# Load order, ScalarE-issued first weight rows and a reordered normalisation loop at the start of an attention plus token-mixing-MLP kernel

## The chip, the cores and the metric

The kernel runs on one core of one Trainium2 chip. The metric is the device time of one execution in microseconds; the number used is the median of several runs. A separate profiled execution gives the trace that is read here. Its span (first to last instruction on the core) is a little shorter than its device time.

## What is computed

The input is `x`, 2048 tokens of 1024 features in bf16. The reference normalises it to `xn`, and returns `x` plus a segmented attention of `xn` (4 segments of 512 tokens, 32 heads, a softmax part and a memory part, mixed by a gate) plus a token-mixing MLP. Only the MLP's first half matters for the change:

```
xn = _layernorm(x, axis=-1)
h  = _layernorm(xn, axis=-1)
u  = jnp.einsum('bsd,sf->bdf', h, w1) + b1      # contraction over the 2048 tokens, f = 3584
u  = gelu(u)
y  = jnp.einsum('bdf,fs->bds', u, w2) + b2
out = x + attention(xn) + transpose(y)
```

Each token's mean and variance over its 1024 features are therefore needed before that token can take part in the first product, and every output of that product needs all tokens.

## The kernel before

Tokens lie on the 128 partitions, in 16 chunks of 128 (`N_TCH`). The work is issued in this order (L571 to L577): `loads`, `warm`, `norm_and_first_hidden`, `hidden`, `over_late`, `attention_and_out`. Engines run their own instruction streams in order; a wait stands in the stream of the engine that waits, so whatever is behind it on that engine waits too.

**First stage (about the first 39 us).** For chunk c the kernel loads `xin[:, c, :]` (256 KB) and the 128 rows of `w1first` that belong to it (512 columns, 128 KB), computes the statistics, writes the normalised `h[:, c, :]`, and runs eight matmuls of 128x512 into eight PSUM banks (4 column blocks of w1, `N_EARLY`, by 2 halves of the features). Chunk c is the c-th term of the contraction, so the matmuls must follow the chunks and TensorE can go no faster than `h` appears.

- `loads` (L715) issues all transfers from SP's queue, in the order they are to land: x0, x1, w1-0, x2, w1-1, x3, w1-2 and 3, x4 and 5, w1-4 and 5, the two bias rows `brow`, and so on in pairs; then `beta_sb` and the first full weight slot `w1slot[2]`. `load_w1` (L743) uses the default issuer of `FW.dma` (L226), which is SP.
- `warm` (L748) clears a tile, lets GpSimd fill `mhalf` with -0.5 (the exponent for the power), runs one tiny gelu on ScalarE, which brings in its table, and lets TensorE run 14 dummy matmuls (`N_WARM`).
- `stats` (L784): the odd chunks (`ACT_STATS`) take their sums on ScalarE, by two passes (L793 mean, L795 mean square). The even chunks take them on VectorE: `bn_stats` of features 0 to 511 (L800, part 0), of 512 to 1023 (L802), and `bn_aggr` (L804), the last two being part 1.
- `scale` (L807): GpSimd turns this into the reciprocal root `ln_r2`: two small operations (L814, L816) and a power (L821) for an odd chunk, one (L819) and the power for an even one. Chunk 0 has L819 on VectorE.
- `ln_h` (L824) on VectorE: `h = (x - mean) * rs` (L829).
- `norm_and_first_hidden` (L761) writes the order out by hand. In each even turn c VectorE's stream is: L800 of chunk c+2, `ln_h(c+1)`, L802 and L804 of chunk c+2, `ln_h(c+2)`. GpSimd's stream is `scale(c+1)`, `scale(c+2)`.
- `bias_columns` (L846) turns the bias rows into columns by eight 32x32 transposes (L851) and a copy (L852), all in one go in turn 10.

**Second stage**, `hidden` (L907), to about 212 us: gelu of the eight early banks on ScalarE (L941), then 48 groups of 16 matmuls for the other 24 column blocks, each with w1 in slots of 256 columns (1 MB). Slots 0 and 1 lie over `w1first` and are loaded once the first stage's last matmuls have read it; slot 2 is used first. In the shade of these matmuls `x` is normalised once more to `xn` and transposed by DMA.

**Third stage**, `attention_and_out`, to the end: its order is set when the program is built, by a planner (`_Flow`) that keeps a clock of its own for every engine and picks the next work by it. The clocks (`FW.now`, `Res.t`) run on from the first instruction of the program, the loads and the first stage included.

Of the kernel before, what the change touches and what calls it, by code (L numbers as in the profile page):

```python
# [6 lines left out]
ACT = mybir.ActivationFunctionType  # L7
# [11 lines left out]
P = 128  # L19
N_TCH = S_TOK // P  # L20
N_DCH = D_MODEL // P
N_FCH = F_MLP // P
# [521 lines left out]
class _Kernel:  # L544
# [169 lines left out]

    def loads(self):  # L715
        fw = self.fw
        self.load_x(0, 1)
        self.load_x(1, 1)
        self.load_w1(0, 1)
        self.load_x(2, 1)  # L720
        self.load_w1(1, 1)
        self.load_x(3, 1)
        self.load_w1(2, 2)
        fw.op("pool", lambda e: e.memset(self.brow[:], 0.0), writes=[self.R_brow, self.R_brow2])
        self.load_x(4, 2)
        self.load_w1(4, 2)
        fw.dma(self.brow[0:N_FCH, :], self.B_b1.rearrange("(c q) -> c q", q=P), reads=[self.R_brow], writes=[self.R_brow])
        fw.dma(self.brow[32:32 + N_TCH, :], self.B_b2.rearrange("(c q) -> c q", q=P), reads=[self.R_brow2],
               writes=[self.R_brow2])
        for c in range(6, 16, 2):  # L730
            self.load_x(c, 2)
            self.load_w1(c, 2)
        fw.dma(self.beta_sb[:], self.A_beta.partition_broadcast(P), writes=[self.R_beta])
        self.w1_srcs = [self.B_w1[:, fp * 256:(fp + 1) * 256].rearrange("(c p) f -> p c f", p=P)
                        for fp in range(N_FCH // 2)]
        fw.dma(self.w1slot[2], self.w1_srcs[2], writes=[self.R_w1s[2]])
        self.w1_next = 3
# [2 lines left out]
        self.fw.dma(self.xin[:, c0:c0 + n, :], self.x_d[:, c0:c0 + n, :],  # L740
                    writes=[self.R_xin[c] for c in range(c0, c0 + n)])

    def load_w1(self, c0, n):  # L743
        self.fw.dma(self.w1first[:, c0:c0 + n, :],
                    self.B_w1[c0 * P:(c0 + n) * P, 0:512].rearrange("(c p) f -> p c f", p=P),
                    writes=[self.R_w1f[c] for c in range(c0, c0 + n)])

    def warm(self):  # L748
        fw = self.fw
        z = self.gT[:, 0, 0:512]  # L750
        R = self.R_gT[0]
        fw.op("dve", lambda e: e.memset(z, 0.0), writes=[R[0]])
        fw.op("pool", lambda e: e.memset(self.mhalf[:], -0.5), writes=[self.R_mhalf])
        fw.op("act", lambda e: e.activation(self.ln_t[:, 0, 0:1], self.mhalf[:, 0:1], ACT.Gelu_apprx_tanh),
              reads=[self.R_mhalf], writes=[self.R_st[0]], ns=1500)
        with fw.group(reads=[R[0]], writes=[self.R_bank[7]], ns=self.N_WARM * 300):
            for _ in range(self.N_WARM):
                fw.mm(self.bank(7), z[:, 0:P], z, start=True, stop=True)


    def norm_and_first_hidden(self):  # L761
        self.stats(0)
        self.scale(0)
        self.stats(1)
        self.ln_h(0, 0)
        self.ln_h(0, 1)
        self.stats(3)
        for c in range(N_TCH):
            self.early_hidden(c)
            if c % 2 == 0:  # L770
                if c + 5 < N_TCH:
                    self.stats(c + 5)
                if c + 2 < N_TCH:
                    self.stats(c + 2, 0)
                self.scale(c + 1)
                self.ln_h(c + 1)
                if c + 2 < N_TCH:
                    self.stats(c + 2, 1)
                    self.scale(c + 2)
                    self.ln_h(c + 2)  # L780
            if c == 10:
                self.bias_columns()

    def stats(self, c, part=None):  # L784
        fw = self.fw
# [57 lines left out]
                fw.mm(self.bank(b), self.w1first[:, c, fc * P:(fc + 1) * P],  # L843
                      self.h[:, c, half * 512:(half + 1) * 512], start=(c == 0), stop=last)

    def bias_columns(self):  # L846
        fw = self.fw
        for i in range(8):
            src = self.brow[32 * (i // 4):32 * (i // 4) + 32, 32 * (i % 4):32 * (i % 4) + 32]
            dst = self.bt[32 * (i % 4):32 * (i % 4) + 32, 32 * (i // 4):32 * (i // 4) + 32]  # L850
            fw.op("dve", lambda e, d=dst, s=src: e.transpose(d, s), reads=[self.R_brow, self.R_brow2], writes=[self.R_bt])  # L851
        fw.op("dve", lambda e: e.tensor_copy(self.bc[:], self.bt[:]), reads=[self.R_bt], writes=[self.R_bc])  # L852

    def later_consts(self):
        fw = self.fw
# [526 lines left out]
```

## Time and profile before

| | us |
|---|---|
| median of 9 runs (700.34 to 700.59) | 700.43 |
| profiled execution, its own time | 700.4 |
| its span | 698.6 |
| TensorE busy, whole span | 689.9 |
| first stage ends (last early matmul) | 39.04 |
| second and third stage | 39.04 to 698.6 |

The granted TensorE clock is at full speed in all slices. The trace is read by stretches: from 39.04 to 212.00 TensorE is busy for 172.96 of 172.96 us, from 212.00 to 450.00 for 237.40 of 238.00 us, from 450.00 to 698.60 for 244.80 of 248.60 us. In the first 39.04 us it has 14 dummy matmuls, 128 real ones and the remaining idle time. Times of instructions below are counted from the span's start.

### The profile page before, as it was taken

How to read it: one execution, taken by the hardware profiler on the slowest of the kernel's cores; microseconds unless marked ns; L12 is line 12 of the kernel's file. 1: busy time of each engine (PE TensorE's matmuls, PEld its weight loads, DVE VectorE, ACT ScalarE, POOL GpSimd, SP SyncE). 2: the span in 40 equal slices, each digit the busy share in tenths (PEclk: the TensorE clock that was granted, in tenths of full speed). 3: DMA queues.
4: the chain of work that ended last, by engine and by line, in shares of the span. 5: the costliest groups of instructions: out<-in, count | busy, mean ns of one | idle time of the engine just before them, and what ended most of it. 6: DMA issues, size and time to landing. Idle time of an engine off the chain costs nothing.

```text
span 698.6 us, 11588 instructions
## 1 busy us (share of the span) xinstructions
PE 689.9 (99%) x4822; PEld 329.0 (47%) x4822; DVE 268.4 (38%) x601; ACT 282.1 (40%) x513; POOL 116.8 (17%) x235
## 2 busy tenths in 40 slices
PE   8899999999999999999999999999999999999997
PEld 3344444444444544445444454544445454444553
DVE  5641100000002433344555564645556463444544
ACT  7331122221135454553545435354543525444350
POOL 3460000000000221221212122121212212121230
PEclk9999999999999999999999999999999999999999
DMA  9365757323019355455272733425263442424204
GB/s 312 111 152 151 183 144 214 109 72 100 1 57 212 84 125 126 88 137 115 60 151 48 149 86 90 115 59 138 59 145 81 94 109 52 116 66 106 50 16 143
DMA packets 211325, 77.32 MB, mean 111 GB/s; under 512 B 173770, under 2 KB 203594, under 8 KB 211274
## 3 DMA queue, kind: packets, MB, share of 16 engines
q1 hardware_dynamic: 211274, 76.59, 44.1%
q8 instruction: 38, 0.62, 0.4%
q14 instruction: 13, 0.11, 0.0%
HBM read 59.79 MB, written 5.24 MB: 93 GB/s over the span
## 4 chain that ended last, share of the span: by engine, by line
PE 94%; DVE 2%; POOL 2%; issue 1%; DMA 1%; ACT 0%; DVEq 0%; POOLq 0%
PE ps_all L217 94%; POOL ln_r L821 1%; DVE ln_st L802 1%; DVE h L829 1%; DMA xin<-in_A_x_dram 0%; POOL ln_t L814 0%; DVE ln_mv L804 0%; DVE bt L851 0%; POOL ln_t L819 0%; POOL ln_t L816 0%; DMA out_dram<-fin 0%; DVE ln_st L800 0%; DVE fin L1243 0%; DVE stg L1331 0%; ACT etmp L951 0%
## 5 line engine op out<-in xcount | busy, mean ns | idle before, releaser
L217 PE MATMUL ps_all<-gT,w2h 128*128 128x512 bf16 x896 | 229.3, 379 | 0.6 <-DVE stg L1331 0.4
L1063 ACT ACTIVATE pT<-ps_all 128x512 bf16<-128x512 f32 x320 | 161.9, 617 | 110.2 <-PE ps_all L217 110.2
L217 PE MATMUL ps_all<-h,w1all 128*128 128x512 bf16 x896 | 194.8, 379 | 3.0 <-DVE h L829 2.8
L1071 POOL TENSOR_SCALAR_AFFINE_SELECT pT<-pT 128x256 bf16<-128x256 bf16 (+3 forms) x176 | 91.5, 525 | 541.6 <-ACT pT L1063 537.7
L217 PEld LDWEIGHTS ps_all<-h,w1all 128*128 128x128 bf16 x896 | 87.1, 98 | 110.7 <-issue 5.4
L217 PEld LDWEIGHTS ps_all<-gT,w2h 128*128 128x128 bf16 x896 | 79.7, 97 | 82.5 <-issue 7.9
L941 ACT ACTIVATE gT<-ps_all,bc 128x512 bf16<-128x512 f32 x56 | 37.7, 690 | 143.9 <-PE ps_all L217 143.9
L1109 DVE CAST ost<-ps_all 128x264 bf16<-128x264 f32 (+1 forms) x128 | 50.5, 396 | 81.9 <-PE ps_all L217 81.3
L217 PEld LDWEIGHTS ps_all<-vA,pT 128*128 128x128 bf16 x1280 | 50.6, 96 | 30.0 <-POOL pT L1071 0.5
L217 PE MATMUL ps_all<-xnT,wk 128*128 128x512 bf16 x256 | 60.5, 379 | 0.0
L217 PE MATMUL ps_all<-xnT,wq 128*128 128x512 bf16 x256 | 60.5, 379 | 0.0
L217 PE MATMUL ps_all<-wv_sb,xnT 128*128 128x512 bf16 x256 | 60.1, 379 | 0.0
L217 PE MATMUL ps_all<-vA,pT 128*128 128x33 bf16 x1280 | 52.0, 178 | 0.0
L968 DVE CAST qT<-ps_all 128x512 bf16<-128x512 f32 x29 | 20.1, 691 | 80.1 <-PE ps_all L217 80.1
L967 ACT ACTIVATE vA<-ps_all 128x512 bf16<-128x512 f32 x18 | 10.8, 599 | 90.6 <-PE ps_all L217 90.6
L879 DVE TENSOR_SCALAR gcol<-gcol 128x32 f32<-128x32 f32 x1 | 0.2, 181 | 118.7 <-ACT gcol L877 118.7
L217 PEld LDWEIGHTS ps_all<-wv_sb,xnT 128*128 128x128 bf16 x256 | 25.1, 98 | 30.2 <-ACT pT L1063 0.2
L217 PEld LDWEIGHTS ps_all<-xnT,wk 128*128 128x128 bf16 x256 | 25.0, 98 | 30.2
L217 PEld LDWEIGHTS ps_all<-xnT,wq 128*128 128x128 bf16 x256 | 25.0, 98 | 30.2 <-issue 0.2
L967 ACT ACTIVATE kT<-ps_all 128x512 bf16<-128x512 f32 x32 | 19.1, 597 | 39.1 <-PE ps_all L217 39.1
L217 PE MATMUL ps_all<-wo_sb,oT 128*128 128x512 bf16 x128 | 34.3, 379 | 0.0
L952 DVE TENSOR_SCALAR etmp<-etmp 128x512 bf16<-128x512 bf16 x48 | 17.6, 367 | 39.8 <-ACT etmp L951 39.7
(68 smaller groups left out, 423.7 us busy)
## 6 DMA issues: line engine op xcount, KB each, us to landing
w2h<-in_B_w_dram SPq DMA_DIRECT2D x64, 224.0 KB, 3.3
w1all<-in_B_w_dram SPq DMA_DIRECT2D x12, 1024.0 KB, 5.2
wq<-in_A_wq_dram SPq DMA_DIRECT2D x32, 256.0 KB, 2.9
wk<-in_A_wk_dram SPq DMA_DIRECT2D x32, 256.0 KB, 2.9
stg<-in_A_x_dram SPq DMA_DIRECT2D x16, 256.0 KB, 3.6
out_dram<-stg SPq DMA_DIRECT2D x16, 256.0 KB, 2.8
xin<-in_A_x_dram SPq DMA_DIRECT2D x6, 512.0 KB, 7.5
wv_sb<-in_A_wv_dram SPq DMA_DIRECT2D x2, 1024.0 KB, 7.8
```

The lines of the kernel that those rows point to most:

```text
L217: ins = self.nc.tensor.matmul(out, *args, **kwargs)
L802: fw.op("dve", lambda e: e.bn_stats(st[:, 6:12], src[:, 512:1024]), reads=[self.R_xin[c], R_t], writes=[R_t], ns=690)
L821: fw.op("pool", lambda e: e.tensor_tensor(rs, t[:, 2:3], self.mhalf[:, 0:1], op=ALU.pow), reads=[self.R_rs[c], self.R_mhalf], writes=[self ...
L829: fw.op("dve", lambda e: e.tensor_scalar(self.h[:, c, a:z], self.xin[:, c, a:z], self.ln_mv[:, c, 0:1], self.ln_r2[:, c:c + 1], op0=ALU.su ...
L879: fw.op("dve", lambda e: e.tensor_scalar(self.gcol[:], self.gcol[:], 1.0, None, op0=ALU.add), reads=[self.R_gcol], writes=[self.R_gcol])
L941: fw.op("act", lambda e: e.activation(self.gT[:, fc, half * 512:(half + 1) * 512], self.bank(b), ACT.Gelu_apprx_tanh, bias=self.b1c[:, fc: ...
L952: fl.op({"dve": (lambda e: e.tensor_scalar(et[:], et[:], 1.0, None, op0=ALU.min), 294, 330)}, [R_et], [R_et], prio=2)
L967: self.flow.op({"act": (lambda e, b: e.activation(dst, view(self.bank(b)), ACT.Copy), 635, 560), "dve": (lambda e, b: e.tensor_copy(dst, v ...
L968: "dve": (lambda e, b: e.tensor_copy(dst, view(self.bank(b))), 690, 727)},
L1063: fl.op({"act": (lambda e, b, slot=slot: e.activation(pT[:, slot, :], self.bank(b), ACT.Exp, scale=SCALE), 620, 530)}, [], [R[slot]], box= ...
L1071: fl.op({"pool": (lambda e, ap=ap, pat=pat: e.affine_select(ap, ap, pattern=pat, compare_op=ALU.is_ge, fill=0.0, base=0, channel_multiplie ...
L1109: fl.op({"dve": (lambda e, b: e.tensor_copy(dst, self.ps[:, b, 0:n * VW]), 150 + n * 35, 185 + n * 35)}, [], [self.R_ost[o][qb]], box=box, ...
```

## The change

It has three parts.

1. **Loads.** x0 to x3 are issued on SP first, one after the other. The w1 rows of chunks 0 to 3 are issued by ScalarE (three transfers, behind the table load and the tiny gelu, which moves here from `warm`). From chunk 4 on, x and w1 pairs follow on SP as before; the bias rows come after the pair 6 and 7. GpSimd fills `mhalf` before it clears `brow`.
2. **Order of the first stage.** In an even turn c VectorE's stream becomes: L802 and L804 of chunk c+2, `ln_h(c+1)`, L800 of chunk c+4, `ln_h(c+2)`. L800 of chunk 2 goes ahead of `ln_h(0)`. GpSimd's stream keeps its order.
3. **Bias columns** come in pieces of two transposes in turns 7, 9, 11 and 13, and the copy in turn 15.

```
     def loads(self):
+        fw.op("pool", lambda e: e.memset(self.mhalf[:], -0.5), writes=[self.R_mhalf])
         fw.op("pool", lambda e: e.memset(self.brow[:], 0.0), writes=[self.R_brow, self.R_brow2])
-        self.load_x(0, 1)
-        self.load_x(1, 1)
-        self.load_w1(0, 1)
-        self.load_x(2, 1)
-        self.load_w1(1, 1)
-        self.load_x(3, 1)
-        self.load_w1(2, 2)
...
-        self.load_x(4, 2)
-        self.load_w1(4, 2)
...
-        for c in range(6, 16, 2):
+        for c in range(4):
+            self.load_x(c, 1)
+        fw.op("act", lambda e: e.activation(self.ln_t[:, 0, 0:1], self.mhalf[:, 0:1], ACT.Gelu_apprx_tanh),
+              reads=[self.R_mhalf], writes=[self.R_st[0]], ns=1500)
+        self.load_w1(0, 1, "act")
+        self.load_w1(1, 1, "act")
+        self.load_w1(2, 2, "act")
+        for c in range(4, 16, 2):
             self.load_x(c, 2)
             self.load_w1(c, 2)
+            if c == 6:
...
     def norm_and_first_hidden(self):
         self.stats(0)
         self.scale(0)
         self.stats(1)
+        self.stats(2, 0)
         self.ln_h(0, 0)
         self.ln_h(0, 1)
-        self.stats(3)
         for c in range(N_TCH):
-            self.early_hidden(c)
             if c % 2 == 0:
-                if c + 5 < N_TCH:
-                    self.stats(c + 5)
-                if c + 2 < N_TCH:
-                    self.stats(c + 2, 0)
-                self.scale(c + 1)
-                self.ln_h(c + 1)
+                if c + 3 < N_TCH:
+                    self.stats(c + 3)
                 if c + 2 < N_TCH:
                     self.stats(c + 2, 1)
+                self.scale(c + 1)
+                if c + 2 < N_TCH:
                     self.scale(c + 2)
+                self.ln_h(c + 1)
+                if c + 4 < N_TCH:
+                    self.stats(c + 4, 0)
+                if c + 2 < N_TCH:
                     self.ln_h(c + 2)
-            if c == 10:
-                self.bias_columns()
+            elif c >= 7:
+                self.bias_columns((c - 7) // 2)
+            self.early_hidden(c)
```

More of the change, by code (lines that the diff above doesn't have):

```diff
@@ L716, in loads @@
         fw = self.fw
-        self.load_x(0, 1)
-        self.load_x(1, 1)
-        self.load_w1(0, 1)
-        self.load_x(2, 1)
-        self.load_w1(1, 1)
-        self.load_x(3, 1)
-        self.load_w1(2, 2)
-        fw.op("pool", lambda e: e.memset(self.brow[:], 0.0), writes=[self.R_brow, self.R_brow2])
-        self.load_x(4, 2)
-        self.load_w1(4, 2)
-        fw.dma(self.brow[0:N_FCH, :], self.B_b1.rearrange("(c q) -> c q", q=P), reads=[self.R_brow], writes=[self.R_brow])
-        fw.dma(self.brow[32:32 + N_TCH, :], self.B_b2.rearrange("(c q) -> c q", q=P), reads=[self.R_brow2],
-               writes=[self.R_brow2])
-        for c in range(6, 16, 2):
+        fw.op("pool", lambda e: e.memset(self.mhalf[:], -0.5), writes=[self.R_mhalf])
+        fw.op("pool", lambda e: e.memset(self.brow[:], 0.0), writes=[self.R_brow, self.R_brow2])
+        for c in range(4):
[6 more added lines that the diff above has]
+        for c in range(4, 16, 2):
             self.load_x(c, 2)
             self.load_w1(c, 2)
+            if c == 6:
+                fw.dma(self.brow[0:N_FCH, :], self.B_b1.rearrange("(c q) -> c q", q=P), reads=[self.R_brow],
+                       writes=[self.R_brow])
+                fw.dma(self.brow[32:32 + N_TCH, :], self.B_b2.rearrange("(c q) -> c q", q=P), reads=[self.R_brow2],
+                       writes=[self.R_brow2])
         fw.dma(self.beta_sb[:], self.A_beta.partition_broadcast(P), writes=[self.R_beta])
@@ L741, in load_x, with load_w1 @@
                     writes=[self.R_xin[c] for c in range(c0, c0 + n)])
-    def load_w1(self, c0, n):
+    def load_w1(self, c0, n, issuer="sp"):
         self.fw.dma(self.w1first[:, c0:c0 + n, :],
                     self.B_w1[c0 * P:(c0 + n) * P, 0:512].rearrange("(c p) f -> p c f", p=P),
-                    writes=[self.R_w1f[c] for c in range(c0, c0 + n)])
+                    writes=[self.R_w1f[c] for c in range(c0, c0 + n)], issuer=issuer)
     def warm(self):
@@ L752, in warm @@
         fw.op("dve", lambda e: e.memset(z, 0.0), writes=[R[0]])
-        fw.op("pool", lambda e: e.memset(self.mhalf[:], -0.5), writes=[self.R_mhalf])
-        fw.op("act", lambda e: e.activation(self.ln_t[:, 0, 0:1], self.mhalf[:, 0:1], ACT.Gelu_apprx_tanh),
-              reads=[self.R_mhalf], writes=[self.R_st[0]], ns=1500)
         with fw.group(reads=[R[0]], writes=[self.R_bank[7]], ns=self.N_WARM * 300):
@@ L844, in early_hidden, with bias_columns @@
                       self.h[:, c, half * 512:(half + 1) * 512], start=(c == 0), stop=last)
-    def bias_columns(self):
+    def bias_columns(self, part):
         fw = self.fw
-        for i in range(8):
+        for i in range(2 * part, min(2 * part + 2, 8)):
             src = self.brow[32 * (i // 4):32 * (i // 4) + 32, 32 * (i % 4):32 * (i % 4) + 32]
             dst = self.bt[32 * (i % 4):32 * (i % 4) + 32, 32 * (i // 4):32 * (i // 4) + 32]
-            fw.op("dve", lambda e, d=dst, s=src: e.transpose(d, s), reads=[self.R_brow, self.R_brow2], writes=[self.R_bt])
-        fw.op("dve", lambda e: e.tensor_copy(self.bc[:], self.bt[:]), reads=[self.R_bt], writes=[self.R_bc])
+            fw.op("dve", lambda e, d=dst, s=src: e.transpose(d, s), reads=[self.R_brow, self.R_brow2],
+                  writes=[self.R_bt])
+        if part == 4:
+            fw.op("dve", lambda e: e.tensor_copy(self.bc[:], self.bt[:]), reads=[self.R_bt], writes=[self.R_bc])
     def later_consts(self):
```

## The prediction

> **What bounds the kernel now.** First I read the busy time by stretches: after 39.04 us TensorE stands still for 0.00, 0.60 and 3.80 us in the three stretches to the end, so nothing is to be had there by an edit of the loads. The rest lies in the first 39.04 us. TensorE's own timeline there (start, duration, operation, idle time before it and who ended it):
>
> ```profile
> 1.25 5.83 PE L217 MATMUL ps_all<-gT 128*128 128x512 bf16 x14 [1.25 <-DVE gT L752]
> 6.92 3.62 PE L217 MATMUL ps_all<-h,w1all 128*128 128x512 bf16 x16
> 10.82 3.61 PE L217 MATMUL ps_all<-h,w1all 128*128 128x512 bf16 x16 [0.28 <-DVE h L829]
> 14.66 3.61 PE L217 MATMUL ps_all<-h,w1all 128*128 128x512 bf16 x16 [0.23 <-DVE h L829]
> 18.48 3.61 PE L217 MATMUL ps_all<-h,w1all 128*128 128x512 bf16 x16 [0.20 <-DVE h L829]
> ...
> 29.93 1.89 PE L217 MATMUL ps_all<-h,w1all 128*128 128x512 bf16 x8 [0.20 <-DVE bt L851]
> 32.88 1.90 PE L217 MATMUL ps_all<-h,w1all 128*128 128x512 bf16 x8 [1.07 <-DVE h L829]
> 35.43 9.87 PE L217 MATMUL ps_all<-h,w1all 128*128 128x512 bf16 x45 [0.65 <-DVE h L829]
> ```
>
> Two chunks take 3.61 us, but a new pair starts only every 3.82 us, and 1.07 + 0.65 us are lost around 32 us. Sixteen chunks at 3.61 / 2 = 1.805 us are 28.88 us; from 6.92 that would end at 35.80. It ends at 35.43 + 3.61 = 39.04 (the last 16 early matmuls). So **3.24 us** stand still, and they are the most that the change can win, as long as TensorE's first real matmul stays at 6.92, where the 14 dummies end.
>
> Next the chain of waits, to see what makes 3.82 (start, duration, what):
>
> ```profile
> 11.51 0.55 DVE h L829
> 12.05 0.61 DVE ln_st L802
> ...
> 12.69 0.22 DVE ln_mv L804
> ...
> 12.99 0.24 POOL ln_t L819
> ...
> 13.30 0.56 POOL ln_r L821
> 13.87 0.30 POOL ln_t L814
> ...
> 14.31 0.27 POOL ln_t L816
> ...
> 14.65 0.58 POOL ln_r L821
> ```
>
> This is a ring: the second half of an even chunk's statistics (L802) stands on VectorE behind `ln_h` of the odd chunk before it, that `ln_h` waits for GpSimd's five operations, and these wait for the statistics. 15.32 - 11.51 = 3.81 us once round, more than TensorE needs. Each engine alone has room: in 10.80 to 14.65 VectorE is busy 2.51 and GpSimd 1.92 us.
>
> Last the transfers. The landing of x4 and x5, issued at 4.09 (KB, us to landing):
>
> ```profile
> xin<-in_A_x_dram SPq DMA_DIRECT2D x1, 512.0 KB, 6.3
> ```
>
> It lands at about 10.4, though ScalarE sits idle for it until 10.43. Taken the same way, one issue at a time, x2 (issued 2.19) lands at 5.7, x3 at 6.9, w1-2/3 at 8.6, x6/7 at 12.4, x8/9 at 14.4, x14/15 at 20.2. The 16 DMA engines are full all that time (share 1.01 in 6.90 to 10.80), so issuing earlier doesn't by itself land earlier.
>
> **What the Trainium skill says.** "DMA: Bandwidth & Descriptors", Queues, rings and completion order: SP and ACT each own a row of rings on the same 16 engines, and an engine goes round-robin between rows with work, a packet at a time. No DMA of ScalarE is in this trace (all loads are on q1), so it is untested here. The same page, Issuing engines are not separate DMA queues: a second issuer saves only issue time; the trace has 0.42 to 0.47 us per issue on SP. "ScalarE: Activation LUTs", What ACT_TABLE_LOAD costs: about 1283 ns; the trace agrees with 1283 ns, and shows no gap after it (the gelu starts at 2.09). "SBUF — State Buffer", Who interferes with whom: a two-port VectorE operation such as `tensor_scalar` can shut GpSimd out for its whole length; L814 at 6.07, beside `ln_h(0)`, took 448 ns against 300 otherwise, which fits.
>
> **Part 2, the order, in the steady state.** Nothing is added; only the order on VectorE moves. In start-to-start times of the trace a pair costs VectorE: `bn_stats` 8.12 to 8.84 = 0.72, twice; `bn_aggr` some 0.24; `ln_h` 10.13 to 10.59 = 0.46, twice: 2 x 0.72 + 0.24 + 2 x 0.46 = 2.60 us. Now L802 waits for no `ln_h` that waits for it, GpSimd's scaling of the even chunk (0.24 + 0.56 and two hops) runs beside `ln_h(c+1)` and L800 of c+4 (0.46 + 0.72), and the odd chunk's scaling needs only ScalarE's sums, done long before (ScalarE needs 2.22 us for a chunk; 17.11 to 19.33). If `ln_h` shuts GpSimd out for its whole 0.55, the turn is 3.15, still below 3.61. So TensorE becomes the bound, and 0.20 a pair goes. What is late next is the arrival of x at about 2.0 us a pair (12.4, 14.4, 16.4), below 3.61 as well.
>
> **Part 3, bias pieces.** The one block of 29.70 to 31.69 on VectorE, 2.0 us, becomes 4 x 0.47 (two transposes at 0.235) and a copy of 0.2. A turn is then 2.60 + 0.47 = 3.07, under 3.61: cost nothing; without that cover it costs 0.47 a piece. The bias rows land some 2 us later than before (about 13); VectorE comes to turn 7 at about 20. The copy is done by about 31, before the first gelu needs it at 35.
>
> **Part 1, loads, and the start.** ScalarE's three issues stand behind the table load and the gelu (end 2.29): 3 x 0.45 gives 3.65, ahead of x1's landing at 4.0, so its statistics of chunk 1 lose nothing. Bounds: below zero, if x1 and x3 land earlier without w1-0 and w1-1 ahead of them (up to 0.55, ScalarE's wait for x3); above, if the two issuers hold each other up, 0.9 each (twice the 0.45), then ScalarE starts at 5.0 and chunk 1's power ends at 8.4 instead of 7.53. I take zero: both ends vanish in the wait below. w1-0 is issued at 2.35 instead of 1.72; with 2.7 us to landing as before and half of the engines' turns, it lands by 5.1 to 6.0, and is needed at 6.92. SP comes to x4/5 at 2.66, and everything moved up on SP waits for nothing.
>
> The step that costs is the new place of L800. L800 of chunk 2 waits for x2 (at most 5.7), so it ends by 6.4, `ln_h(0)` half 0 at 6.8, half 1 at 7.25: TensorE starts at 6.92 still. L802, L804 and `ln_h(1)` follow to 8.75; chunk 1 is wanted at 8.72, 0.1 late at most. Then **L800 of chunk 4 stands ahead of `ln_h(2)`**, and waits for x4/5. The 2 MB up to and with x4/5 are the same as before: in turns, 32 packets a DMA engine of x2 to x5 go against 32 of w1-0 to 3, so both end together, at the landing of before, 10.4, or a little earlier as the w1 rows trail by up to 0.6 us. Below: 9.4, if ScalarE's rows are held back. Above: 11.4, if the rate stays 10% lower with two rings. I take 10.2. Then L800 starts at 10.2, `ln_h(2)` at 10.92, and TensorE 0.69 after its start (10.13 to 10.82 before): **11.61**, against 10.82 before and 10.53 wanted. Here a stall of 1.08 us is added.
>
> From there no step is late: L802, L804, `ln_h(3)`, L800 of chunk 6 (x6/7 at 12.4) and `ln_h(4)` end at 14.2, and chunk 4 is wanted at 15.22; the lead grows by about 1 us a pair. Fourteen chunks x 1.805 = 25.27: the stage ends at 36.88 instead of 39.04, **2.16 us** earlier. After it, slot 2 of w1 has long landed (24.0), slots 0 and 1 are loaded 2.16 earlier and used 14.4 us after that (landing took 5.3 and 7.1), bank 0 is free after the first gelu. TensorE is full to 212, so all shifts. The planner's clocks at its start are set by TensorE's 48 groups, so I expect the same order, shifted.
>
> Sum against the profiled execution's own 700.4: 700.4 - 2.16 = 698.24; the median stands 0.03 above that run, so **698.3**.
>
> **Rivals.** (1) x4/5 lands by 9.5 or ScalarE's rows are late: the wait disappears, and the whole 3.24 is won, 697.2. For: a second queue of work in the engines; against: they are full. Chance 0.17. (2) The gain is half lost: x4/5 only at 11.4 or later (each us costs one), or the planner, with other clock values, picks another order; 699.4 to 700.4. Against: the clocks only shift. Chance 0.13. (3) Slower: ScalarE's ring is starved. SP now has all of x and the other w1 rows queued; were its ring served first, w1-0 would come after x14/15 (20.2), at about 20.9, and the stage would end at 20.9 + 28.9 = 49.8: 711.2. It decides as soon as w1-0 lands after 39.04 - 28.88 = 10.16, or w1-2/3 after 39.04 - 25.27 = 13.77. Against: round-robin, as above. Chance 0.07. (4) That the order doesn't come out as written is excluded: the streams are emitted in program order. The forecast (10.2, within 9.5 to 10.9; 697.5 to 699.0) has 0.63.
>
> **From these the numbers.** Forecast and (1) are faster: 0.80; (2) is within 0.2% (1.4 us, about what a measurement of this kernel can tell from no change): 0.13; slower 0.07. Range: 697.1, (1) with 0.1 for the measurement, to 699.4, the upper bound of the landing.
>
> **What would show it.** TensorE in 16 chunks without a gap from chunk 2 on; one gap of about 1.1 us before chunk 2, ended by L829 behind an L800 that waited for x4/5; last early matmul at 36.9; no L851 in the chain; stretches after it unchanged. Wrong, if TensorE waits for w1, if gaps of 0.2 remain, or if TensorE's idle time in the attention part moves from 4.4 us.

## The result, and the profile after

| | before | after |
|---|---|---|
| median, us | 700.41 (29 runs) | 696.58 (9 runs, 696.11 to 696.84) |
| ratio, 95% interval | | 0.9944 [0.9936, 0.9953] |
| profiled execution, own time / span | 700.4 / 698.6 | 696.58 / 694.7 |
| first matmul of the first stage | 6.92 | 7.42 |
| end of the first stage, by matmul starts | 38.88 | 35.04 |
| from there to the end of the span | 659.7 | 659.7 |

The change wins 3.83 us; the forecast was 2.1, and the fastest time in its range, 697.1, lies 0.5 above the result. A tenth run on record beside these nine took 697.63, and the same kernel took 697.20 and 697.62 in two later sessions (gains of 3.20 and 2.80 there), inside the range. The profile read in this section is the one of 696.58. TensorE's own timeline of the kernel after, in the first 45 us (start, duration, operation, idle time before it and what ended it):

```profile
1.25 5.46 PE L217 MATMUL ps_all<-gT 128*128 128x512 bf16 x14 [1.25 <-DVE gT L753]
7.42 37.93 PE L217 MATMUL ps_all<-h,w1all 128*128 128x512 bf16 x175 [0.71 <-DVE h L829]
```

The breaks between pairs, and the two around 32 us, are gone: one unbroken row of matmuls runs from 7.42 on. It also gives the pace, the time from the start of one matmul to the start of the next. A matmul is shown for 0.379 us (its end is modelled, and overlaps the next matmul), so 175 of them in 37.93 us start every (37.93 - 0.38) / 174 = **0.216 us**. The rows of before show the same: (3.61 - 0.38) / 15 = 0.215 within a pair, (9.87 - 0.38) / 44 = 0.216 in the last group. A chunk of eight is therefore 1.727 us, not the 1.805 of the prediction, and the first stage takes 128 x 0.2158 = 27.62 us when nothing breaks it. Its end counts as the start of the matmul after it: 35.43 + 16 x 0.2158 = 38.88 before, 7.42 + 27.62 = 35.04 after. The difference, 3.84, is the whole gain.

The same is seen from the other side, in the stretches of the kernel after from there to the end (length, busy time and number of matmuls, then weight loads, VectorE, ScalarE, GpSimd, clock, DMA share and GB/s):

```profile
39.04:212.00 172.96, 172.96 (x803) 78.38 (x801) 9.56 (x21) 38.28 (x58) 0.00 (x0) 1.00 0.47 128
212.00:450.00 238.00, 237.40 (x1927) 116.15 (x1926) 110.35 (x262) 113.42 (x213) 44.90 (x88) 1.00 0.49 107
450.00:694.70 244.70, 240.96 (x1938) 118.50 (x1935) 121.43 (x260) 105.96 (x201) 46.63 (x88) 1.00 0.36 88
```

TensorE stands still for 0.00, 0.60 and 3.74 us (0.00, 0.60 and 3.80 before). TensorE's 4822 matmuls write and read the same tiles in the same order in both traces, so on TensorE the planner did only shift.

What holds the start is shown by the chain of waits of the kernel after (start, duration, what):

```profile
1.73 4.52 DMA xin<-in_A_x_dram
...
6.27 0.69 DVE ln_st L800
6.96 0.32 DVE h L829
...
7.42 4.69 PE ps_all L217 x21
```

The transfer issued at 1.73 is x2. L800 of chunk 2, the first half of that chunk's statistics, waits for it until 6.27, with `ln_h(0)` behind it on VectorE. The ring of L802, GpSimd and `ln_h` is no longer in the chain, and neither are L851 and x4/5. VectorE after the start, in the kernel after:

```profile
8.24 0.21 DVE L804 BATCH_NORM_AGGREGATE ln_mv<-ln_st 128x2 f32<-128x12 f32 x1
8.37 0.53 DVE L829 TENSOR_SCALAR h<-xin,ln_mv,ln_r 128x1024 bf16<-128x1024 bf16 x1
9.52 0.70 DVE L800 BATCH_NORM_STATS2 ln_st<-xin 128x6 f32<-128x512 bf16 x1 [0.62 <-DMA xin<-in_A_x_dram]
10.13 0.53 DVE L829 TENSOR_SCALAR h<-xin,ln_mv,ln_r 128x1024 bf16<-128x1024 bf16 x1
10.57 0.69 DVE L802 BATCH_NORM_STATS2 ln_st<-xin 128x6 f32<-128x512 bf16 x1
...
13.10 0.69 DVE L802 BATCH_NORM_STATS2 ln_st<-xin 128x6 f32<-128x512 bf16 x1
...
15.84 0.69 DVE L802 BATCH_NORM_STATS2 ln_st<-xin 128x6 f32<-128x512 bf16 x1
...
19.03 0.69 DVE L802 BATCH_NORM_STATS2 ln_st<-xin 128x6 f32<-128x512 bf16 x1
...
22.29 0.69 DVE L802 BATCH_NORM_STATS2 ln_st<-xin 128x6 f32<-128x512 bf16 x1
```

L800 of chunk 4 does wait for x4/5, as forecast, but until 9.52 and not 10.2. `ln_h(2)` starts at 10.13, TensorE could take chunk 2 at 10.13 + 0.69 = 10.82, and it wants it at 7.42 + 2 x 1.727 = 10.87: the wait is just covered. The distance between the L802 is VectorE's turn for two chunks: 2.53 and 2.74 us without a bias piece, 3.19 and 3.26 with one (forecast: 2.60 and 3.07). TensorE needs 3.45 for two chunks, so VectorE now gets ahead of it.

### The profile page after: what moved, and what is told of

It reads as the page before. It is cut to its first block, busy times and chain, and to the rows that moved or that the text cites. A ratio compares the mean times of both kernels' runs of the same rounds, so it can differ in the third digit from the quotient of the medians.

```text
span 694.7 us, 11589 instructions
## 1 busy us (share of the span) xinstructions
PE 688.4 (99%) x4822; PEld 329.3 (47%) x4822; DVE 268.1 (39%) x601; ACT 281.9 (41%) x513; POOL 118.3 (17%) x235
## 4 chain that ended last, share of the span: by engine, by line
PE 98%; DMA 1%; DVE 0%; ACT 0%; issue 0%; SPq 0%; DVEq 0%
PE ps_all L217 98%; DMA xin<-in_A_x_dram 1%; DMA out_dram<-fin 0%; DVE fin L1245 0%; SPq L245 0%; DVE stg L1333 0%; DVE ln_st L800 0%; ACT etmp L953 0%; ACT vA L969 0%; ACT kT L969 0%; DVE h L829 0%; DVE etmp L954 0%; DVEq L65 0%; DVE pkT L956 0%
```

## The experiments

The theory after the result: TensorE's pace is 0.216 us in both kernels, the change wins by opening the ring, all in the first stage, and what is left is set by landings at the start (x2, x4/5). The rivals: TensorE itself ran slower before, the loads are the source, or the bias block is. Each ratio is to runs of the kernel before in the same session (medians 700.42, 700.56, 700.40 and 700.42, in this order of the four headings below). A break in TensorE's row is given as the profile draws it; counted from start to start, 0.16 us more is lost, as a matmul is drawn 0.379 long and the next could have started after 0.216.

**One part at a time.** `late_start`, against the kernel before:

```
-    N_WARM = 14
+    N_WARM = 33
```

> The kernel before with 33 dummy matmuls instead of 14: 19 more at 0.216 us let TensorE's first real matmul start at about 11.0 instead of 6.92, while h comes as before. Pace theory (matmuls start every 0.216 us, so a chunk is 1.727 us and the 3.61 of a pair holds 0.16 us of pipeline end that costs nothing): chunks 0 to 13 end by 11.0 + 14 x 1.727 = 35.2, before the last wait ends at 35.43, so the time stays: 700.4, within 0.2. The prediction's 1.805 us a chunk (or the rival that TensorE itself runs slower before the change than after it): 11.0 + 25.3 = 36.3, 0.9 us slower: 701.3.

Measured: 700.39 (ratio 1.0000 [0.9991, 1.0008]). The time says less than was expected of it: the dummies ended earlier, so that the start was at 9.80, where 1.805 a chunk would also have been ready in time (9.80 + 25.3 = 35.1). The timeline decides:

```profile
9.80 22.61 PE L217 MATMUL ps_all<-h,w1all 128*128 128x512 bf16 x102
32.81 1.90 PE L217 MATMUL ps_all<-h,w1all 128*128 128x512 bf16 x8 [0.40 <-DVE h L829]
35.36 9.87 PE L217 MATMUL ps_all<-h,w1all 128*128 128x512 bf16 x44 [0.65 <-DVE h L829]
```

Thirteen chunks (104 matmuls, two records missing) take 22.61 = 13 x 1.727 + 0.16; at 1.805 they would take 23.5. With the order of before and 2.9 us more delay at the start, TensorE catches up with VectorE and ends at the same time. The pace theory holds, and TensorE was not slower before.

`order_only`: the new `norm_and_first_hidden`, with the loads of before and the bias block in one piece (the lines are against the new loop):

```
-            elif c >= 7:
-                self.bias_columns((c - 7) // 2)
             self.early_hidden(c)
+            if c == 10:
+                self.bias_columns()
```

> Only the new order of the first stage, with the loads of before and the bias columns in one block in turn 10. Pace theory with two waits at the start: TensorE starts at 6.95, x4/5 lands at 10.4 as before, so L800 of chunk 4 holds ln_h(2) and chunk 2 starts at 11.8; 11.8 + 14 x 1.727 = 36.0 against 38.88 before: 697.5, with the bias block hidden. If the loads don't matter: as the full change, 696.6. If the gain came from the loads: 700.4.

Measured: 697.43 (697.15 to 697.86; ratio 0.9958 [0.9945, 0.9970]). Its TensorE:

```profile
7.51 3.61 PE L217 MATMUL ps_all<-h,w1all 128*128 128x512 bf16 x16 [1.11 <-DVE h L831]
11.67 33.61 PE L217 MATMUL ps_all<-h,w1all 128*128 128x512 bf16 x152 [0.55 <-DVE h L831]
```

The order alone wins 3.0 us, beside 3.8, 3.2 and 2.8 of the full change in its three sessions. The bias block in one piece leaves no break: VectorE is far enough ahead by turn 10. The break before chunk 2 is there, as x4/5 lands at 10.4 with the loads of before; the start is later than expected, as x2 came late in this execution (L800 of chunk 2 at 6.35).

`loads_only`: the new `loads` and `warm`, all else as in the kernel before.

> Only the new loads, with the order and the bias block of before. Pace theory: the ring of L802, GpSimd and ln_h still sets 3.82 us a pair, and it is entered later, since x1 lands later than before (4.3 against 4.0), so ScalarE's sums of chunk 1 and all behind them come some 0.3 us later: 700.7. If earlier loads were the source of the gain that the prediction missed: 699 or less.

Measured: 701.03 (ratio 1.0009 [1.0001, 1.0017]), slower by 0.6. The pairs still start every 3.82 us (15.38, 19.20, 23.01 in its profile); the ring is entered later. The loads are not the source.

`bias_only`, against the kernel before:

```
-            if c == 10:
-                self.bias_columns()
+            if c % 2 and c >= 7:
+                self.bias_columns((c - 7) // 2)
```

> Only the bias columns in pieces, with the loads and order of before. The block costs 5.50 - 3.82 = 1.7 us before. In the ring a piece of 0.47 has 0.2 us of cover (VectorE's idle time ahead of ln_h of the odd chunk), so four pieces cost about 4 x 0.27 = 1.1: 699.8. If a piece is hidden altogether: 698.7. If it costs its whole length: 700.6.

Measured: 699.42 (ratio 0.9986 [0.9980, 0.9993]), a gain of 1.0 by itself. Its pairs start at 22.33, 26.31, 30.42 and 34.52, so a turn with a piece takes 3.98 to 4.11 instead of 3.82: a piece costs 0.16 to 0.29, in the mean 0.24, near the 0.27 expected. In the new order this gain isn't added, since there the block is hidden as well.

**Where the start and chunk 2 are held.** All edits from here on are against the kernel after. `act_waits` (`load_w1` hands the list on as `extra=` to `FW.dma`):

```
-        fw.op("act", lambda e: e.activation(self.ln_t[:, 0, 0:1], ...
+        gelu = fw.op("act", lambda e: e.activation(self.ln_t[:, 0, 0:1], ...
-        self.load_w1(0, 1, "act")
+        self.load_w1(0, 1, "act", [gelu])
```

> The full change, but ScalarE's three w1 transfers wait for the end of its small gelu (2.30), so they are issued at about 2.35 to 3.7, as the prediction had assumed, instead of 0.95 to 2.31. x2 then has fewer w1 rows beside it and lands by 5.7 or before: TensorE starts at 6.95 instead of 7.42. Chunk 2 then waits for L800 of chunk 4, which starts when x4/5 lands. If a second ring is what made x4/5 land at 9.5: chunk 2 at 10.8, stage end 35.0, 696.5. If the early issue did it, x4/5 lands at 10 or later: chunk 2 at 11.4, stage end 35.6, 697.1. The prediction's own stall at x4/5 = 10.2: chunk 2 at 11.6, 697.3.

Measured: 697.39 (696.76 to 699.06; ratio 0.9958 [0.9944, 0.9972]). A new wait took the place of the old: w1-0, issued at 2.33, landed only at 8.2, and TensorE's row reads

```profile
8.23 37.08 PE L217 MATMUL ps_all<-h,w1all 128*128 128x512 bf16 x168 [1.18 <-DMA w1all<-in_B_w_dram]
```

x2 was earlier (L800 of chunk 2 at 5.93), x4/5 unchanged (9.51).

`x4_alone`:

```
-            self.load_x(c, 2)
+            if c == 4:
+                self.load_x(4, 1)
+                self.load_x(5, 1)
+            else:
+                self.load_x(c, 2)
```

> The full change with x4 and x5 as two transfers instead of one. L800 of chunk 4 then needs only x4, some 0.7 us earlier than x4/5 together. Two equal waits: the start at 7.42 (x2, L800 of chunk 2 ahead of ln_h of chunk 0) and chunk 2 (x4/5). With one of them gone, the other still sets the end: 696.5, within 0.2 of the full change. If x4/5 alone sets it: 696.0.

Measured: 697.59 (696.31 to 698.07; ratio 0.9954 [0.9941, 0.9967]), no gain. L800 of chunk 4 started at 9.21 without a wait, L800 of chunk 2 at 6.46, TensorE at 7.61. With the wait for x4/5 gone, x2 still sets the end of this profiled execution (696.87).

`act_waits_x4_alone`: both edits.

> Both edits at once: w1 rows of ScalarE behind its gelu, and x4 and x5 apart. Two equal waits: both go, TensorE starts at 6.95 and runs 16 x 1.727 = 27.63 us without a gap, stage end 34.6 instead of 35.04: 696.1. If x4 still comes after 9.2, chunk 2 waits and it is 696.3 to 696.8.

Measured: 696.67 (696.08 to 697.08; ratio 0.9946 [0.9932, 0.9960]). In the profiled execution (696.08) w1-0 landed at 6.90, and TensorE ran from 6.94 without a break.

`half_behind`:

```
                 self.ln_h(c + 1)
-                if c + 4 < N_TCH:
-                    self.stats(c + 4, 0)
                 if c + 2 < N_TCH:
                     self.ln_h(c + 2)
+                if c + 4 < N_TCH:
+                    self.stats(c + 4, 0)
```

> The full change, but in each even turn L800 of chunk c+4 stands behind ln_h(c+2) instead of ahead of it; what remains of the new order is that L802 and bn_aggr stand ahead of ln_h(c+1). A turn of VectorE is then 2 x 0.72 + 0.24 + 0.98 (the wait for GpSimd's 0.80 and two hops, ln_h(c+1) inside it) + 0.46 = 3.1, still below 3.45: no gap in the steady state, and ln_h(2) no longer stands behind x4/5. The start at 7.42 sets the end: 696.5. If the half ahead is what opens the ring: gaps return in every pair, 699 or more.

Measured: 698.40 (697.59 to 698.84; ratio 0.9968 [0.9957, 0.9980]), well above the 696.5 expected. Part of it is the start, 8.59, as x2 came at 7.4. The rest is VectorE's turn:

```profile
12.95 0.53 DVE L829 TENSOR_SCALAR h<-xin,ln_mv,ln_r 128x1024 bf16<-128x1024 bf16 x1
13.13 0.44 POOL L819 TENSOR_SCALAR ln_t<-ln_mv 128x1 f32<-128x1 f32 x1 [0.98 <-DVE ln_mv L804]
...
13.65 0.57 POOL L821 TENSOR_TENSOR ln_r<-ln_t,mhalf 128x1 f32<-128x1 f32 x1
...
14.33 0.55 DVE L829 TENSOR_SCALAR h<-xin,ln_mv,ln_r 128x1024 bf16<-128x1024 bf16 x1 [0.84 <-POOL ln_r L821]
```

From one `ln_h(c+1)` to the next `ln_h(c+2)` are 1.38 us, not the 0.98 expected. About half of the difference is L819, which takes 0.44 beside `ln_h` instead of 0.23; the rest is the time between the operations (0.18, 0.08 and 0.11 in these lines). The turn is 14.33 - 10.91 = 3.42, just below TensorE's 3.45; with a bias piece it goes over (3.71 and 3.85), and TensorE has one drawn break of 0.62 at 32. So opening the ring is enough to go from 3.82 to 3.42, and the half put ahead, with which the turn is 2.53 to 2.74, fills the remaining wait: it makes the lead that hides the bias columns.

**A session with the full change in it.** `after_again`, the full change unchanged:

> The full change once more, as a yardstick for the three edits beside it: 696.6, with single times spread over about 1 us, since x2's landing (5.8 to 7.4 in the profiles so far) sets TensorE's start.

Measured: 697.20 (696.80 to 697.46; ratio 0.9953 [0.9939, 0.9967]). L800 of chunk 2 at 6.91, TensorE at 8.06, no wait for x4/5.

`split_first`:

```
-        self.stats(2, 0)
         self.ln_h(0, 0)
+        self.stats(2, 0)
         self.ln_h(0, 1)
```

> The full change with L800 of chunk 2 between the two halves of ln_h(0) instead of ahead of both. TensorE's first four matmuls need only the first half, so they start at 6.95 whenever x2 lands; the second half is wanted at 7.8, which holds if x2 lands by 6.6. Start theory: the x2 wait goes, and chunk 2 behind x4/5 (9.3 to 9.8, plus 1.4) is what remains, 10.7 to 11.2 against 10.9 in the full change: 696.6, with a smaller spread. If the start alone set the end: 696.1.

Measured: 697.12 (696.38 to 697.26; ratio 0.9950 [0.9937, 0.9963]). x2 came at 7.25, later than the 6.6 that the edit can bear: TensorE started at 7.09, broke for 0.20 at the second half of chunk 0 and for 0.35 at chunk 1, behind the same L800.

`x4_alone_again`:

> The kernel with x4 and x5 apart, again, beside the full change of the same group. Start theory: x2 sets the end in both, so both are the same within 0.3. If it was 1 us slower than the full change for a reason of its own: 697.6 against 696.6.

Measured: 697.62 (697.15 to 697.84; ratio 0.9959 [0.9946, 0.9972]), 0.4 above the full change of its session, with overlapping intervals. L800 of chunk 2 at 6.85, TensorE at 8.00.

`split_first_x4`: both edits.

> Both: L800 of chunk 2 between the halves of ln_h(0), and x4 and x5 apart. Start theory: neither wait is left, TensorE runs from 6.95 for 27.63 us without a gap, stage end 34.6: 696.1, 0.5 below the full change of the same group. If a late w1-0 or another wait takes their place: 696.6.

Measured: 697.22 (696.45 to 697.50; ratio 0.9953 [0.9939, 0.9967]), not the 696.1 expected: x2 at 7.44, breaks of 0.25 and 0.35 as in `split_first`. The "two equal waits" were wrong. In the profiled executions of these kernels x2 alone sets the end, even with its L800 one place further back.

**Why x2 is late.** `after_third`, the full change again:

> The full change as the yardstick of this group: 696.6 to 697.2, TensorE's start in the profile 1.2 us after x2's landing, 7.4 to 8.1.

Measured: 697.62 (14 runs, 696.27 to 699.59; ratio 0.9967 [0.9958, 0.9976]). L800 of chunk 2 at 6.77, TensorE at 7.92. Five of the times lie between 699.3 and 699.6. These five list a mean granted clock of 0.998, the other nine 0.999 or 1.0 (and the 699.06 of `act_waits` lists 0.998). 0.2% of 697 us is 1.4 us, an estimate of what the clock adds there; the rest of these five isn't explained. Without them the median is 697.53.

`w10_early` (with `gelu` named as in `act_waits`):

```
         self.load_w1(0, 1, "act")
-        self.load_w1(1, 1, "act")
+        self.load_w1(1, 1, "act", [gelu])
```

> The full change, with w1-0 issued by ScalarE at once and w1-1 and w1-2/3 only behind its gelu (2.3). x2 theory: the later rows no longer stand ahead of x2, which lands at 5.7 or before; w1-0 lands by 4; TensorE starts at 6.95, and chunk 2 then waits for x4/5 (9.4 + 1.4): 10.8 at the latest against 10.4 wanted: 696.2 to 696.6. If x2 is late for another reason (a slow DMA engine): start at 7.4 or later, as the full change.

Measured: 697.00 (696.70 to 697.03; ratio 0.9949 [0.9936, 0.9962]). L800 of chunk 2 at 6.12, TensorE at 7.28, and a break of 0.10 (0.26 from start to start) before chunk 2, behind x4/5 at 9.70: now this wait does show.

`w10_early_x4`: the same with x4 and x5 apart.

> The same with x4 and x5 apart. x2 theory: neither wait is left, TensorE runs from 6.95 without a gap to 34.6: 696.1. If w1-2/3, now later, is late for chunk 2 (it must land by 10.4): 696.4.

Measured: **696.55** (695.99 to 696.89; ratio 0.9943 [0.9930, 0.9956]). Its TensorE and VectorE:

```profile
7.06 38.15 PE L217 MATMUL ps_all<-h,w1all 128*128 128x512 bf16 x173
```

```profile
5.49 0.69 DVE L804 BATCH_NORM_STATS2 ln_st<-xin 128x6 f32<-128x512 bf16 x1
6.10 0.72 DVE L833 TENSOR_SCALAR h<-xin,ln_mv,ln_r 128x512 bf16<-128x512 bf16 x2
```

L804 is L800 of the other kernels, moved by four lines. It waits for nothing, TensorE starts as the dummies end, and nothing breaks it; the chain of this kernel's first 14 us holds TensorE alone after the dummies' memset. In its session all five times lie below the median of the full change (697.62); in another session the full change itself had 696.58, so no lasting gain over it is shown.

`act_waits_x4_again`:

> All of ScalarE's rows behind its gelu, x4 and x5 apart, again. x2 lands at 5.7, but w1-0 may land at 7 to 8 and then sets TensorE's start: 696.1 if by 6.9, 697.2 if at 8. Median as before, 696.7; w10_early_x4 should lie below it, since there only w1-0 is early.

Measured: 696.85 (696.62 to 697.03; ratio 0.9948 [0.9935, 0.9961]). L800 of chunk 2 at 6.64, w1-0 at 7.2, TensorE at 7.79.

Over all nine profiles of kernels whose first stage is unbroken, the profiled time is the start of the first matmul plus 689.1 to 689.3: for instance 7.42 and 696.58, 8.06 and 697.20, 7.92 and 697.10, 8.23 and 697.39, 7.06 and 696.21. And with L800 of chunk 2 ahead of `ln_h(0)`, the start is that L800 plus 1.15 wherever it waited for x2 and w1-0 came no later (w1-0 came later in `act_waits` and `act_waits_x4_alone`).

Why x2 is late is seen one level deeper. A transfer lands in 16 parts: the traces have 16 increments of its semaphore, and the engine that waits goes on at the last one. For x2 (us):

| profile | 8th part | 15th part | last part |
|---|---|---|---|
| before | 5.40 | 5.67 | 5.70 |
| `order_only` (loads of before) | 5.30 | 6.06 | 6.33 |
| full change, three sessions | 5.41, 5.37, 5.34 | 5.53, 5.65, 5.98 | 6.25, 6.88, 6.75 |
| `w10_early`, `w10_early_x4` | 5.14, 5.09 | 5.42, 5.35 | 6.10, 5.46 |
| `act_waits`, `_x4_alone`, `_x4_again` | 4.80, 4.66, 4.76 | 5.77, 5.13, 6.13 | 5.91, 5.62, 6.62 |

The middle of the transfer follows the order of issue: 0.2 to 0.3 us earlier than in the full change with two of the three w1 transfers held back, 0.5 to 0.8 with all three. The last part trails the middle by 0.27 to 1.96 us over the 18 profiles, differently in every execution, and in the full change by 0.84, 1.51 and 1.41. This is what moves TensorE's start. Why a part is late isn't shown; nor is it shown that the new loads make it later, as their 14 profiles (0.37 to 1.96) overlap the four with the loads of before (0.27 to 1.03).

## Why the prediction was wrong

The direction, the place and the mechanism were right: the ring was the bound, it is gone, all of the gain lies in the first stage, the bias pieces are hidden, TensorE's order only shifted. The size was wrong, and the sentence that failed first is "Sixteen chunks at 3.61 / 2 = 1.805 us are 28.88 us", with "**3.24 us** stand still, and they are the most that the change can win".

| term | predicted | measured | moves the gain by |
|---|---|---|---|
| first stage before ends | 39.04 | 38.88 | -0.16 |
| start of TensorE | 6.92 | 7.42 | -0.50 |
| break before chunk 2 | 1.08 | 0.00 | +1.08 |
| 16 chunks | 28.88 | 27.62 | +1.26 |
| first stage after ends | 36.88 | 35.04 | |
| gain | 2.16 | 3.84 | +1.68 |

The terms of the start and of the break belong together. Had TensorE started at 6.92 with x4/5 as it came, it would have wanted chunk 2 at 10.37 and got it at 10.82, an estimated stall of 0.45: the late start hid most of a break that was still there. And that the two later sessions, at 697.20 and 697.62, lie inside the forecast's range is luck: there too TensorE ran at 0.216 us a matmul, and its start at 8.06 and 7.92 gave back part of what the pace had left out.

- **The pace.** 3.61 is the length of a group as the profile draws it, the last matmul's 0.379 included; when the next group follows at once, 0.16 of that lies under its first matmul. What stood still in a pair was 3.82 - 3.45 = 0.37, not 0.20, and in all 38.88 - 6.92 - 27.62 = 4.34 us. The group of 45 in the prediction's own timeline (9.87) would have told it. So would the Trainium skill, "TensorE: Matmul & The Clock Gate", Wait — 56ns, not 53.3ns?: it gives 215.7 ns from start to start for 512 columns once warm; the trace has 215.8. `late_start` shows the pace within the kernel before. So the first rival's 3.24, "the whole", was too small as well.
- **The break before chunk 2.** "L800 of chunk 4 stands ahead of `ln_h(2)`" was right as a mechanism: `order_only` has that break, 0.55, with x4/5 at 10.4. In the full change x4/5 landed at 9.49, which is the condition of the first rival ("x4/5 lands by 9.5", chance 0.17), and L800 starts at 9.52. By the prediction's own steps chunk 2 could then be taken at 9.52 + 0.72 + 0.69 = 10.93 (10.82 measured). Against the 1.08 forecast the earlier landing takes 0.68 and the late start of TensorE the rest. The landing is the term that was mis-sized: x4/5 came at 10.18 to 10.41 in the four profiles with the loads of before, and at 9.17 to 9.85 in the eight where the new loads bring it as one transfer. In these two profiles the DMA stretches of 6 to 10 us carry more than before (before, then after; in front of the last column, GB/s, stands the share of the DMA engines):

```profile
6.00:8.00 2.00, 2.00 (x9) 0.81 (x8) 1.68 (x4) 1.45 (x4) 1.21 (x3) 1.00 1.03 294
8.00:10.00 2.00, 2.00 (x11) 0.94 (x10) 1.01 (x3) 1.29 (x4) 0.78 (x2) 1.00 0.98 331
```

```profile
6.00:8.00 2.00, 1.29 (x7) 0.42 (x6) 1.73 (x4) 0.88 (x2) 1.34 (x4) 1.00 1.01 352
8.00:10.00 2.00, 2.00 (x11) 0.88 (x9) 1.35 (x4) 1.79 (x3) 1.34 (x4) 1.00 1.05 375
```

  352 and 375 GB/s instead of 294 and 331, at about the same share of the engines. "the 16 DMA engines are full ... so issuing earlier doesn't by itself land earlier" took a busy engine for one at its rate. But the rate alone doesn't bring x4/5 in: `bias_only`, with the loads of before, moved 365 and 354 GB/s in these stretches, and the last part of x4/5 still came at 10.28. Whether the second queue or the earlier issue (x4/5 at 2.66 instead of 4.09) does it isn't settled, since they came together in every run.
- **The start.** "ScalarE's three issues stand behind the table load and the gelu (end 2.29)" was wrong: the trace has them at 0.95 to 2.31, while the table is loaded (0.80 to 2.08), and all three begin ahead of the gelu (2.10). The w1 rows so moved ahead of x2. Against holding them back this costs the middle of x2 0.5 to 0.8 us, about what x2's own earlier issue (1.73 instead of 2.19) had won: its 8th part landed as before (5.41 against 5.40), so this alone doesn't make TensorE late. The step that failed is "waits for x2 (at most 5.7)", a bound taken from one execution. In the full change 15 of its 16 parts were there by 5.53 and the last came at 6.25, 6.88 and 6.75; in `order_only`, with the old loads, at 6.33.
- **w1-0**, issued at 2.35, "lands by 5.1 to 6.0": `act_waits` issued it at 2.33, and it landed at 8.2 (6.9 and 7.2 in the two other profiles of such kernels). The turns of the two queues, on which the estimate rests, are there: from 3 to 5 us of the full change the trace counts 283 packets of SP's queue and 291 of ScalarE's, in `act_waits` 240 and 193 from 5 to 7 us. What the estimate left out are the last parts again: in `act_waits` the 8th part of w1-0 landed at 6.31, the 14th at 6.64, and the last two at 7.66 and 8.19. The third rival, a starved ScalarE queue, was not seen: in the full change w1-0 landed at 3.85 and w1-2/3 at 8.34.
- **The parts.** With the order new, the other two parts bring little: `order_only` is at 697.43, the full change at 696.58, 697.20 and 697.62 in three sessions. What the loads and the pieces are worth on top of the order lies between a gain of 0.85 and a loss of 0.2, and isn't settled beyond that.

## What to carry to other kernels

Take an engine's pace from the distance between starts in its longest unbroken group, not from a short group's length divided by its count; the end that a profile draws for the last one turns into a bound that isn't there. When two engines hand work to each other in a ring, put the next item's first half and everything that needs no answer between question and answer, so that no instruction waits behind one that waits for it. Once such a ring is open, the landing of the first inputs sets the time and its spread: the kernel before ranged over 0.4 to 0.5 us in a session, the one after over 0.7 to 1.9 (without the runs at a lower clock). A landing read in one execution is no upper bound, as the last of 16 parts decides: read it in several before a sum rests on it.

## What was not expected of the hardware

- ScalarE issued three DMAs (0.95 to 2.31 us) while its table was loading (0.80 to 2.08), though they stand behind the gelu that needs the table.
- In the full change 15 of x2's 16 parts were there at 5.53 us and the last at 6.25; in `half_behind` the 8th came at 5.45 and the last four at 7.25 to 7.41.
- Two kinds of operation of VectorE differ for GpSimd beside them. L819 took 0.23 us while VectorE stood still (before), and 0.41 to 0.49 in the full change where it began 0.14 us or more into an `ln_h`; there it ended 0.08 to 0.10 us after that `ln_h`, whenever it had begun. L814 took 0.31 beside `bn_stats`, and 0.30 in the ring of before. This agrees with the lock that "SBUF — State Buffer" describes in Who interferes with whom.
- The same 14 dummy matmuls took 4.60 to 6.14 us in the profiles, as the distance between their starts changes from 0.427 to 0.216 us at another moment in every execution; in the kernel before and in `w10_early_x4`, where the inputs were in time, this set TensorE's start.
